# The last three and first two key tiles of a group summed bank by bank, and token ids and half of the first z loaded on ScalarE's queue

## The chip, the cores and the metric

The kernel runs on one core of a Trainium2 chip. The metric is the device time of one execution in microseconds (us). The kernel before takes 3062.32 us, the median of three runs (3061.7 to 3063.84). The execution that was profiled took 3063.57 us; its trace spans 3061.9 us.

## The reference

A gated attention unit feeds a hash-routed mixture of experts. All arrays are float32, except the token ids (int64).

```python
# u, v: (8, 2496, 256); z: (8, 2496, 64)
scores = (1.0 / S) * np.matmul(z, z.transpose(0, 2, 1))
attn = np.maximum(scores, 0.0) ** 2
x = (u * np.matmul(attn, v)).reshape(B * S, D)

expert_idx = token_ids * 2654435761 % 8
for e in range(8):
    mask = expert_idx == e
    h = np.maximum(x[mask] @ w1[e], 0.0)     # w1[e]: 256 x 1024
    out[mask] = h @ w2[e]                    # w2[e]: 1024 x 256
```

## The kernel before

**Stages.** The first 1836 us are the attention, the rest are the experts. The order of instructions on every engine is the order of the program's text; no scheduler changes it.

**Attention.** A batch has 2496 rows: 19 key tiles of 128 rows and a last one of 64. Queries go in groups of four tiles, five groups to a batch, 40 groups in all. For one group, `scores` (L131) multiplies z by itself for one key tile (L136, one matmul of 512 columns), ScalarE and VectorE take turns with the ReLU (L141, L139) and write the tile `a`, and VectorE squares `a` in place (`square`, L145, operation L148). `attend` (L160, matmul L162) then multiplies one 128-column piece of `a` by the 256 columns of `v` and adds it into `acc`. The scores of a group come in two parts: the first in the group before, just ahead of that group's last key tiles, the second at its own tile 7. The short key tile has a function of its own (`attend_last`, L157).

**The accumulators.** `acc` is two tiles of 128 x 2 x 256 floats, each one bank of PSUM, and there are two buffers for all groups. Queries q = 0 and 1 share the first bank, q = 2 and 3 the second. Once all 20 key tiles are added for a query, `gate` (L165, operation L171) has VectorE read its half of the bank, scale it, multiply it by `u` and write `x_sb`; after the fourth, GpSimd stores the rows to `x_rows` in device memory (L103).

**The end of a group.** Key tiles 0 to 15 are added for all four queries, tile by tile. For the last three (`LATE = 3`) the order turns round, query by query:

```python
for q in range(G):
    for t, a in late:
        attend(b, t, a, acc, [q])
    gate(b, g, q, acc)
    square(2)
    if q:
        between()
```

Matmuls and gates on one bank wait for each other: a gate waits for its query's last matmul, and the next matmul into that bank waits for the gate.

**The routing.** `places` (L187) works out from the token ids where each token goes. It is a generator; `between` (L342), called after every key tile, runs one step of it, so its VectorE operations sit between the squares. Its first step loads the ids to `tok` (L193, L194) on SyncE's queue, its mask (L224) feeds six small matmuls `cnt_ps` (L238) on TensorE, and a scan over 1280 columns follows (L243).

**Start of the program.** SyncE's queue issues, in this order: z of batch 0 twice, once into each half of `zn` (`load_z`, L108, six transfers), v and u of batch 0, z and v of batch 1 (`zn` has one buffer, so this waits for the transposes of batch 0), then the token ids. TensorE transposes z (L128), ScalarE copies the results to `zT` (L129), and the first scores follow.

**Experts.** Rows are gathered from `x_rows` (L414), multiplied by w1 and w2 (L433, L444) and scattered to the output (L447).

Of the kernel before, what the change touches and what calls it, by code (L numbers as in the profile page):

```python
# [12 lines left out]
I32 = mybir.dt.int32  # L13
# [11 lines left out]
def kernel(  # L25
# [10 lines left out]
    nc = tc.nc  # L36

    B, S, D = u.shape
    K = z.shape[-1]
    N = B * S  # L40
    E, _, F = moe_w1.shape
# [3 lines left out]
    P = 128  # L45
    TM = S // P
    SM = TM * P
    R = S - SM
    T = TM + 1
    assert R == 64 and K == 64  # L50
    G = 4
# [10 lines left out]
    def pool(name, bufs, **kw):  # L62
        return ctx.enter_context(tc.tile_pool(name=name, bufs=bufs, **kw))

    const = pool("const", 1)
# [19 lines left out]
    def width(t):  # L85
        return P if t < TM else R

    def group(g):
        return range(g * G, min(T, g * G + G))

    def tiles_io(dram, b, tiles, sb, store, eng, twice=False):

        rows = dram[ds(b * S, S), :]
        whole = [t for t in tiles if t < TM]
        pairs = []
        if whole:
            n = len(whole)
            pairs.append((rows[0:SM, :].rearrange("(p t) d -> p t d", t=TM)[:, ds(whole[0], n), :], sb[:, 0:n, :]))
        if TM in tiles:
            for i in range(2 if twice else 1):  # L100
                pairs.append((rows[SM:S, :], sb[ds(i * R, R), len(whole), :]))
        for d, s in pairs:
            eng.dma_start(out=d if store else s, in_=s if store else d)  # L103

    uf, vf, zf = (x.rearrange("b s d -> (b s) d") for x in (u, v, z))
    zn, zT, v_sb, u_sb, x_sb, made, to_square = {}, {}, {}, {}, {}, {}, []

    def load_z(b):  # L108
        zn[b] = npool.tile([P, T, 2, K], F32, name="zn")
        for i in range(2):  # L110
            tiles_io(zf, b, range(T), zn[b][:, :, i, :], False, nc.sync, twice=True)

    def load_v(b):
        v_sb[b] = vpool.tile([P, T, D], F32, name="v_sb")
        for g in range(NG):
            tiles_io(vf, b, group(g), v_sb[b][:, g * G:, :], False, nc.sync, twice=True)

    def load_u(b, g):
        u_sb[b, g] = upool.tile([P, G, D], F32, name="u_sb")
        tiles_io(uf, b, group(g), u_sb[b, g], False, nc.sync)  # L120

    def turn_z(b, g):

        if g == 0:
            zT[b] = zpool.tile([P, T * P], F32, name="zT")
        ps = mm_ps.tile([P, G * P], F32, name="z_ps", tag="mm")
        for i, t in enumerate(group(g)):
            nc.tensor.transpose(ps[:, ts(i, P)], zn[b][:, t].rearrange("p h k -> p (h k)"), ident[:])  # L128
        nc.scalar.copy(zT[b][:, ts(g, G * P)], ps[:])  # L129
# [15 lines left out]
    def square(n):  # L145
        for key in to_square[:n]:
            a = made[key]
            nc.vector.tensor_mul(a[:], a[:], a[:])  # L148
        del to_square[:n]
# [10 lines left out]
    def attend(b, t, a, acc, queries):  # L160
        for i in queries:
            nc.tensor.matmul(acc[i // 2][:, i % 2, :], a[:, ts(i, P)], v_sb[b][:, t, :],  # L162
                             start=(t == 0 and i % 2 == 0), stop=(t == TM - 1), skip_group_check=True)

    def gate(b, g, i, acc):  # L165
        q = g * G + i
        m = width(q)
        if i == 0:
            x_sb[b, g] = xpool.tile([P, G, D], F32, name="x_sb")
        x = x_sb[b, g]  # L170
        nc.vector.scalar_tensor_tensor(  # L171
            out=x[0:m, i, :], in0=acc[i // 2][0:m, i % 2, :], scalar=c2, in1=u_sb[b, g][0:m, i, :],
            op0=OP.mult, op1=OP.mult,
        )
        if i == G - 1:
            tiles_io(x_dram, b, group(g), x, True, nc.gpsimd)
# [7 lines left out]
    token = const.tile([P, B, T], I32)  # L184
    none = const.tile([P, NS], I32)

    def places():  # L187

        with tc.tile_pool(name="route", bufs=1) as route:
            tok_h = dataclasses.replace(moe_token_ids.tensor, shape=list(moe_token_ids.tensor.shape))  # L190
            tok_w = tok_h.bitcast(I32).rearrange("(b s two) -> b s two", b=B, two=2)
            tok = route.tile([P, B, T, 2], I32)
            nc.sync.dma_start(tok[:, :, 0:TM, :], tok_w[:, 0:SM, :].rearrange("b (p t) two -> p b t two", t=TM))  # L193
            nc.sync.dma_start(tok[0:R, :, TM, :], tok_w[:, SM:S, :].rearrange("b p two -> p b two"))  # L194

            iota_e = route.tile([P, E], F32)
            nc.gpsimd.iota(iota_e[:], pattern=[[1, E]], base=0, channel_multiplier=0,
                           allow_small_or_imprecise_dtypes=True)
# [29 lines left out]

            total = route.tile([P, E, C], F32)
            rank = route.tile([P, E, C], F32)
            H = 512 // C
# [87 lines left out]
    def slots_to_read():  # L321

        nc.vector.tensor_scalar(gidx[:], idx[:], float(N - 1), None, op0=OP.min)

    order = tc.manual_schedule()
    order.__enter__()

    load_z(0)
    load_v(0)
    load_u(0, 0)  # L330
    for g in range(NG):
        turn_z(0, g)

    LATE = 3
    parts = [[TM, *range(T // 2 - 1)], [*range(T // 2 - 1, TM)]]
    groups = [(b, g) for b in range(B) for g in range(NG)]
    place = places()
    i = 0  # L340

    def between():  # L342

        nonlocal i
        if i < 2 * T:
            next(place, None)
        elif i % 4 == 0 and i < 2 * T + 4 * C:
            enter((i - 2 * T) // 4)
        elif i == 2 * T + 4 * C + T:
            slots_to_read()  # L350
        i += 1
# [4 lines left out]
    for n, (b, g) in enumerate(groups):  # L356
        if n + 1 < len(groups):
            load_u(*groups[n + 1])
        if g == 0 and b + 1 < B:
            load_z(b + 1)  # L360
            load_v(b + 1)
            turns = iter(range(NG))

        def turn():
            k = next(turns, None) if g and b + 1 < B else None
            if k is not None:
                turn_z(b + 1, k)

        acc = [acc_ps.tile([P, 2, D], F32, name="acc", tag="acc") for _ in range(2)]
        for t in range(TM - LATE):  # L370
            if t == T // 2 - LATE:
                turn()
                scores(b, g, parts[1])
                attend_last(b, made.pop((b, g, TM)), acc)
                square(2)
                between()
            attend(b, t, made.pop((b, g, t)), acc, range(G))
            square(2)
            between()
        turn()  # L380
        if n + 1 < len(groups):
            scores(*groups[n + 1], parts[0])
        square(1)
        late = [(t, made.pop((b, g, t))) for t in range(TM - LATE, TM)]
        for q in range(G):
            for t, a in late:
                attend(b, t, a, acc, [q])
            gate(b, g, q, acc)
            square(2)
            if q:  # L390
                between()
    assert next(place, None) is None and i > 2 * T + 4 * C + T


# [104 lines left out]
```

## Time and profile before

| what | value |
|---|---|
| median of three runs | 3062.32 us |
| time of the profiled execution | 3063.57 us |
| its span | 3061.9 us |
| TensorE busy | 2981.1 us (97%) |
| VectorE busy | 1017.9 us (33%) |
| ScalarE busy | 428.1 us (14%) |
| GpSimd busy | 548.9 us (18%) |
| granted TensorE clock, mean | 0.996 |

In the trace one float32 matmul is two records of TensorE: the 40 x 76 calls of L162 are 6080 records. PE is TensorE's matmuls, PEld its weight loads, DVE is VectorE, ACT ScalarE, POOL GpSimd, and SPq is SyncE's queue of DMA issues. Ends of matmuls are modelled, so the time between two starts tells more than a group's own length. The granted clock is 1.00 at 2.4 GHz and 0.50 at 1.2 GHz.

### The profile page before, as it was taken

What the parts mean: (1) busy time and instruction counts of PE and PEld (TensorE: products, weight loads), DVE (VectorE), ACT (ScalarE), POOL (GpSimd) and SP (SyncE); (2) the same over time, 40 slices, a digit from 0 to 9 for tenths busy, and PEclk for the clock granted to TensorE, in tenths of its full rate; (3) what the DMA queues carried; (4) which work ended last, traced back from release to release, by engine and by line L of the source; (5) the groups of instructions that cost most, each with busy time, mean ns of one, the idle gap of its engine ahead of it and who ended that gap; (6) DMA issues with size and microseconds to landing.
All of it is one profiled execution on the core that took longest, in us unless ns stands there. A gap on an engine that the chain in (4) does not pass through costs nothing.

```text
span 3061.9 us, 33981 instructions
## 1 busy us (share of the span) xinstructions
PE 2981.1 (97%) x13946; PEld 2412.0 (79%) x13946; DVE 1017.9 (33%) x1649; ACT 428.1 (14%) x781; POOL 548.9 (18%) x564
## 2 busy tenths in 40 slices
PE   7999999999999999999999999999999999999999
PEld 5777777777777777777777778888888888888888
DVE  5544344454444444444445441111111111111111
ACT  1111111111111111111111111111111111111111
POOL 0011111011011011011100002223223222222232
PEclk9999999999999999999999999999999999999999
DMA  4011011011011011011000204545545545555453
GB/s 127 27 45 55 20 45 62 14 45 62 14 45 61 14 45 61 14 45 62 26 17 27 102 13 137 198 175 183 193 171 190 186 175 197 178 180 196 172 189 98
DMA packets 195547, 295.99 MB, mean 97 GB/s; under 512 B 59484, under 2 KB 148205, under 8 KB 195392
## 3 DMA queue, kind: packets, MB, share of 16 engines
q1 hardware_dynamic: 168400, 230.43, 23.1%
q0 software_dynamic: 26992, 63.39, 5.6%
q8 instruction: 110, 1.80, 0.2%
q14 instruction: 45, 0.37, 0.0%
HBM read 252.69 MB, written 42.90 MB: 97 GB/s over the span
## 4 chain that ended last, share of the span: by engine, by line
PE 64%; issue 24%; POOL 7%; DVE 3%; SPq 1%; DMA 1%; POOLq 0%; DVEq 0%
PE acc L162 40%; PE s_ps L136 11%; PE h_ps L433 6%; PE o_ps L444 5%; POOL xg L414 4%; POOL out_dram L447 3%; DVE x_sb L171 2%; DVE a L148 1%; PE acc L157 1%; SPq L103 1%; PE z_ps L128 0%; PE x_ps L423 0%; DMA tok<-in_moe_token_ids_dram 0%; POOLq L447 0%; DMA v_sb<-in_v_dram 0%
## 5 line engine op out<-in xcount | busy, mean ns | idle before, releaser
L162 PE MATMUL acc<-v_sb,a 128*128 128x256 f32 x6080 | 1357.3, 382 | 52.2 <-DVE x_sb L171 50.8
L162 PEld LDWEIGHTS acc<-v_sb,a 128*128 128x128 f32 x6080 | 1142.9, 190 | 277.3 <-DVE x_sb L171 82.9
L433 PE MATMUL h_ps<-xT,w 128*128 128x256 f32 x2720 | 617.0, 380 | 0.8 <-issue 0.8
L444 PE MATMUL o_ps<-w,hT 128*128 128x256 f32 x2720 | 614.5, 379 | 0.0
L139 DVE TENSOR_SCALAR a<-s_ps 128x512 f32<-128x512 f32 x400 | 276.6, 691 | 923.3 <-PE s_ps L136 923.3
L444 PEld LDWEIGHTS o_ps<-w,hT 128*128 128x128 f32 x2720 | 516.8, 190 | 70.3
L433 PEld LDWEIGHTS h_ps<-xT,w 128*128 128x128 f32 x2720 | 511.6, 191 | 67.7 <-issue 1.2
L148 DVE TENSOR_TENSOR a<-a 128x512 f32<-128x512 f32 x800 | 501.0, 683 | 0.0
L439 DVE TENSOR_SCALAR hT<-h_ps 128x512 f32<-128x512 f32 x170 | 117.6, 692 | 767.5 <-PE h_ps L433 767.5
L136 PE MATMUL s_ps<-zT 64*128 64x512 f32 x1600 | 365.6, 600 | 0.7 <-ACT zT L129 0.7
L141 ACT ACTIVATE a<-s_ps 128x512 f32<-128x512 f32 x400 | 238.8, 597 | 907.7 <-PE s_ps L136 907.7
L447 POOL DMA_INDIRECT out_dram<-o_sb,idx x170 | 170.7, 1004 | 819.8 <-ACT o_sb L446 807.8
L103 POOL DMA_DIRECT2D x_rows<-x_sb x48 | 27.7, 578 | 1582.3 <-DVE x_sb L171 1582.3
L136 PEld LDWEIGHTS s_ps<-zT 64*128 64x128 f32 x1600 | 148.3, 187 | 172.9 <-issue 171.7
L414 POOL DMA_INDIRECT xg<-x_rows,gidx x170 | 174.8, 1028 | 57.1 <-PE h_ps L433 28.5
L312 POOL DMA_INDIRECT slot_tokens<-token,addr x160 | 171.9, 1074 | 48.8 <-issue 48.8
L446 ACT COPY o_sb<-o_ps 128x256 f32<-128x256 f32 x170 | 63.2, 372 | 775.6 <-PE o_ps L444 775.6
L425 DVE COPY xT<-x_ps 128x512 f32<-128x512 f32 x85 | 58.8, 692 | 268.1 <-PE x_ps L423 268.1
L437 ACT ACTIVATE hT<-h_ps 128x512 f32<-128x512 f32 x170 | 101.5, 597 | 304.8 <-PE h_ps L433 269.6
L129 ACT COPY zT<-z_ps 128x512 f32<-128x512 f32 x40 | 23.3, 585 | 641.1 <-PE z_ps L128 641.1
L171 DVE SCALAR_TENSOR_TENSOR x_sb<-acc,u_sb 128x256 f32<-128x256 f32 (+1 forms) x160 | 67.6, 423 | 57.3 <-PE acc L162 57.3
L423 PE MATMUL x_ps<-ident,xg 128*128 128x128 f32 x340 | 51.8, 275 | 6.5 <-DMA xg<-x_rows,gidx 6.5
(54 smaller groups left out, 190.8 us busy)
## 6 DMA issues: line engine op xcount, KB each, us to landing
w<-in_moe_w_dram SPq DMA_DIRECT2D x170, 1024.0 KB
v_sb<-in_v_dram SPq DMA_DIRECT2D x32, 512.0 KB
u_sb<-in_u_dram SPq DMA_DIRECT2D x32, 512.0 KB
x_rows<-x_sb POOLq DMA_DIRECT2D x32, 512.0 KB
zn<-in_z_dram SPq DMA_DIRECT2D x16, 608.0 KB
v_sb<-in_v_dram SPq DMA_DIRECT2D x8, 384.0 KB
u_sb<-in_u_dram SPq DMA_DIRECT2D x8, 384.0 KB
x_rows<-x_sb POOLq DMA_DIRECT2D x8, 384.0 KB
```

The lines of the kernel that those rows point to most:

```text
L136: nc.tensor.matmul(ps[:], zT[b][h, ts(t, P)], zT[b][h, ts(g, G * P)], start=True, stop=True)
L139: nc.vector.tensor_scalar_max(a[:], ps[:], 0.0)
L141: nc.scalar.activation(a[:], ps[:], AF.Relu)
L148: nc.vector.tensor_mul(a[:], a[:], a[:])
L162: nc.tensor.matmul(acc[i // 2][:, i % 2, :], a[:, ts(i, P)], v_sb[b][:, t, :], start=(t == 0 and i % 2 == 0), stop=(t == TM - 1), skip_gro ...
L171: nc.vector.scalar_tensor_tensor(out=x[0:m, i, :], in0=acc[i // 2][0:m, i % 2, :], scalar=c2, in1=u_sb[b, g][0:m, i, :], op0=OP.mult, op1= ...
L312: st = nc.gpsimd.indirect_dma_start(out=slot_dram[:, None], out_offset=bass.IndirectOffsetOnAxis(ap=addr[0:n, c:c + 1], axis=0), in_=token ...
L414: nc.gpsimd.indirect_dma_start(out=xg[j][t][:], out_offset=None, in_=x_dram[:, :], in_offset=bass.IndirectOffsetOnAxis(ap=gidx[:, j * TB + ...
L433: nc.tensor.matmul(ps[:, i, :], w1[j][:, c, ts(f + i, P)], xT[j][:, c, :], start=(c == 0), stop=(c == DP - 1))
L439: nc.vector.tensor_scalar_max(o, ps[:], 0.0)
L444: nc.tensor.matmul(ps[:], hT[j][:, f, ts(t, P)], w2[j][:, f, :], start=(f == 0), stop=(f == FP - 1))
L447: st = nc.gpsimd.indirect_dma_start(out=out[:], out_offset=bass.IndirectOffsetOnAxis(ap=idx[:, j * TB + t:j * TB + t + 1], axis=0), in_=o[ ...
```

## The change

The last three key tiles are added in two passes, one for each bank: three tiles for queries 0 and 1, their two gates, then three tiles for queries 2 and 3 and their gates. The first two key tiles of the next group (`EARLY = 2`) are added in the same way, both tiles for queries 0 and 1, then both for 2 and 3. `square(1)` ahead of the last tiles becomes `square(3)`. The token ids are loaded right behind the first loads, on ScalarE's queue, and so is the second copy of z of batch 0. `places` gets six empty steps ahead of its first matmul.

```diff
-            tiles_io(zf, b, range(T), zn[b][:, :, i, :], False, nc.sync, twice=True)
+            tiles_io(zf, b, range(T), zn[b][:, :, i, :], False, nc.scalar if i and not b else nc.sync, twice=True)
...
+    def load_tokens():
...
+        nc.scalar.dma_start(tok[:, :, 0:TM, :], tok_w[:, 0:SM, :].rearrange("b (p t) two -> p b t two", t=TM))
+        nc.scalar.dma_start(tok[0:R, :, TM, :], tok_w[:, SM:S, :].rearrange("b p two -> p b two"))
...
-            nc.sync.dma_start(tok[:, :, 0:TM, :], tok_w[:, 0:SM, :].rearrange("b (p t) two -> p b t two", t=TM))
-            nc.sync.dma_start(tok[0:R, :, TM, :], tok_w[:, SM:S, :].rearrange("b p two -> p b two"))
...
+            for _ in range(6):
+                yield
             total = route.tile([P, E, C], F32)
...
     load_u(0, 0)
+    load_tokens()
...
+    EARLY = 2
     LATE = 3
...
-        for t in range(TM - LATE):
+        early = [(t, made.pop((b, g, t))) for t in range(EARLY)]
+        for k in range(2):
+            for t, a in early:
+                attend(b, t, a, acc, [2 * k, 2 * k + 1])
+            square(2)
+            between()
+        for t in range(EARLY, TM - LATE):
...
-        square(1)
+        square(3)
+
         late = [(t, made.pop((b, g, t))) for t in range(TM - LATE, TM)]
-        for q in range(G):
+        for k in range(2):
             for t, a in late:
-                attend(b, t, a, acc, [q])
-            gate(b, g, q, acc)
+                attend(b, t, a, acc, [2 * k, 2 * k + 1])
+            for q in (2 * k, 2 * k + 1):
+                gate(b, g, q, acc)
             square(2)
-            if q:
-                between()
+            between()
+        between()
```

**A group's end, TensorE.** One row here is one matmul of the program (two records in the trace), `x12` is twelve of them, and the words in brackets are what the first of them waits for (DVE: VectorE). Before, the 12 matmuls of the last three tiles and the first tiles of the next group stand so:

```order
L162 MATMUL acc<-v_sb,a 128x256 x3
L162 MATMUL acc<-v_sb,a 128x256 [waits DVE_49]
L162 MATMUL acc<-v_sb,a 128x256 x5
L162 MATMUL acc<-v_sb,a 128x256 [waits DVE_49]
L162 MATMUL acc<-v_sb,a 128x256 x4
L162 MATMUL acc<-v_sb,a 128x256 [waits DVE_49]
L162 MATMUL acc<-v_sb,a 128x256 x25
```

Now:

```order
L162 MATMUL acc<-v_sb,a 128x256 x12
L162 MATMUL acc<-v_sb,a 128x256 [waits DVE_49]
L162 MATMUL acc<-v_sb,a 128x256 x3
L162 MATMUL acc<-v_sb,a 128x256 [waits DVE_49]
L162 MATMUL acc<-v_sb,a 128x256 x15
```

The waits of query 1 and query 3 are gone from among the twelve; the waits for VectorE now stand ahead of the next group's first four matmuls (first bank) and its second four (second bank).

**The same place, VectorE.** The rows are the last ReLUs (L139), squares (L148) and gates (L171). Before, in the third group:

```order
L139 TENSOR_SCALAR a<-s_ps 128x512 x5
L148 TENSOR_TENSOR a<-a 128x512
L171 SCALAR_TENSOR_TENSOR x_sb<-acc,u_sb 128x256
L148 TENSOR_TENSOR a<-a 128x512 x2
L171 SCALAR_TENSOR_TENSOR x_sb<-acc,u_sb 128x256
L148 TENSOR_TENSOR a<-a 128x512 x2
L171 SCALAR_TENSOR_TENSOR x_sb<-acc,u_sb 128x256
L148 TENSOR_TENSOR a<-a 128x512 x2
L171 SCALAR_TENSOR_TENSOR x_sb<-acc,u_sb 128x256
L148 TENSOR_TENSOR a<-a 128x512 x3
```

Now in the very first group, where the routing's steps run too (L247 is the scan, L250 and L252 an addition and a subtraction over 1280 columns):

```order
L139 TENSOR_SCALAR a<-s_ps 128x512 x5
L148 TENSOR_TENSOR a<-a 128x512 x3
L171 SCALAR_TENSOR_TENSOR x_sb<-acc,u_sb 128x256 x2
L148 TENSOR_TENSOR a<-a 128x512 x2
L247 SCALAR_TENSOR_TENSOR upto<-ones,total 128x1280
L171 SCALAR_TENSOR_TENSOR x_sb<-acc,u_sb 128x256 x2
L148 TENSOR_TENSOR a<-a 128x512 x2
L250 TENSOR_TENSOR rank<-rank,upto 128x1280
L252 TENSOR_TENSOR rank<-rank,total 128x1280
```

The gates come in pairs with two squares between the pairs. In the first group alone the scan has moved between the pairs; it stood ahead of that group's last ReLUs before.

**The start, TensorE and ScalarE.** TensorE before:

```order
L136 MATMUL s_ps<-zT 128x512 x10
L162 MATMUL acc<-v_sb,a 128x256 x24
L238 LDWEIGHTS all_230
L238 MATMUL cnt_ps<-mask,all_230 128x480
L162 MATMUL acc<-v_sb,a 128x256 x4
L238 LDWEIGHTS below
L238 MATMUL cnt_ps<-mask,below 128x480
L136 MATMUL s_ps<-zT 128x512 x10
```

Now:

```order
L136 MATMUL s_ps<-zT 128x512 x10
L162 MATMUL acc<-v_sb,a 128x256 x28
L136 MATMUL s_ps<-zT 128x512 x10
L157 MATMUL acc<-v_sb,a 128x256 x4
L162 MATMUL acc<-v_sb,a 128x256 x16
L242 LDWEIGHTS all_230
L242 MATMUL cnt_ps<-mask,all_230 128x480
```

And ScalarE now, whose first instruction was the table load before:

```order
L103 DMA zn<-in_z_dram 128x19x64
L103 DMA zn<-in_z_dram 64x64 x2
L192 DMA tok<-in_moe_token_ids_dram 128x8x38
L193 DMA tok<-in_moe_token_ids_dram 64x8x2 [waits DMAHW0_49]
L129 ACT_TABLE_LOAD
L129 COPY zT<-z_ps 128x512 [waits PE_49] x5
```

The first routing matmul moves from behind 24 matmuls of L162 to behind 44 and the second part of the scores. ScalarE issues five transfers ahead of its table load and its first copy, and the fifth waits for an earlier transfer, the first of z.

## Rows read from the trace of the kernel before

**Rows 1.** Windows of the two stages: PE, PEld, DVE, ACT, POOL busy, clock, DMA, GB/s.
```profile
60.00:1836.00 1776.00, 1724.85 (x7983) 1312.91 (x7981) 812.65 (x1351) 253.31 (x425) 199.67 (x208) 1.00 0.13 40
1836.00:3061.90 1225.90, 1214.69 (x5780) 1068.36 (x5780) 176.40 (x256) 164.74 (x340) 346.11 (x341) 1.00 0.50 176
```
**Rows 2.** Who waited for whom: us in total, times, longest.
```profile
PE acc L162 <- DVE x_sb L171: 50.8, 80, 0.8
```
**Rows 3.** Timeline of TensorE over one group: start, us, what, [idle before it].
```profile
250.17 1.56 PE L162 MATMUL acc<-v_sb,a 128*128 128x256 f32 x6
...
269.45 4.56 PE L136 MATMUL s_ps<-zT 64*128 64x512 f32 x20
...
274.80 15.81 PE L162 MATMUL acc<-v_sb,a 128*128 128x256 f32 x72
290.54 4.56 PE L136 MATMUL s_ps<-zT 64*128 64x512 f32 x20
```
**Rows 4.** Timeline of TensorE and VectorE at the end of a later group.
```profile
1788.49 1.56 PE L162 MATMUL acc<-v_sb,a 128*128 128x256 f32 x6
...
1789.24 0.68 DVE L148 TENSOR_TENSOR a<-a 128x512 f32<-128x512 f32 x1
1790.09 0.42 DVE L171 SCALAR_TENSOR_TENSOR x_sb<-acc,u_sb 128x256 f32<-128x256 f32 x1 [0.17 <-PE acc L162]
...
1790.57 2.86 PE L162 MATMUL acc<-v_sb,a 128*128 128x256 f32 x12 [0.52 <-DVE x_sb L171]
...
1793.71 0.42 DVE L171 SCALAR_TENSOR_TENSOR x_sb<-acc,u_sb 128x256 f32<-128x256 f32 x1
1794.04 1.28 DVE L148 TENSOR_TENSOR a<-a 128x512 f32<-128x512 f32 x2
...
1794.18 13.65 PE L162 MATMUL acc<-v_sb,a 128*128 128x256 f32 x62 [0.76 <-DVE x_sb L171]
```
**Rows 5.** Timeline of TensorE at the last group's end.
```profile
1813.12 17.10 PE L162 MATMUL acc<-v_sb,a 128*128 128x256 f32 x78
...
1834.11 1.56 PE L162 MATMUL acc<-v_sb,a 128*128 128x256 f32 x6 [0.52 <-DVE x_sb L171]
```
**Rows 6.** Timeline of the start, all engines.
```profile
0.82 1.28 ACT L129 ACT_TABLE_LOAD   x1 [0.82 <-PEq L485]
...
9.37 3.76 PE L128 MATMUL z_ps<-ident,zn 128*128 128x128 f32 x20 [9.37 <-DMA zn<-in_z_dram]
...
12.20 1.60 ACT L129 COPY zT<-z_ps 128x512 f32<-128x512 f32 x3 [0.27 <-PE z_ps L128]
...
19.84 10.63 PE L162 MATMUL acc<-v_sb,a 128*128 128x256 f32 x48 [1.42 <-DVE a L148]
...
28.09 1.70 SPq L194 DMA_DIRECT2D tok<-in_moe_token_ids_dram  x1
...
37.43 0.56 PE L238 MATMUL cnt_ps<-mask,all 128*128 128x480 bf16 x1 [6.97 <-DVE mask L224]
...
46.71 1.03 PE L157 MATMUL acc<-v_sb,a 64*128 64x256 f32 x8
...
49.60 0.37 PE L238 MATMUL cnt_ps<-mask,below 128*128 128x480 bf16 x1
...
55.50 2.81 DVE L243 TENSOR_TENSOR_SCAN upto<-ones,total 128x1280 f32<-128x1280 f32 x1
```
**Rows 7.** Chain that ended last, SyncE's issue of the second z.
```profile
4.18 0.60 SPq L103
```
**Rows 8.** Windows of the start; the last three columns: granted clock, DMA share, GB/s.
```profile
2.00:9.37 7.37, 0.00 (x0) 0.03 (x1) 0.00 (x0) 0.11 (x1) 1.80 (x5) 1.00 0.99 193
5.00:6.00 1.00, 0.00 (x0) 0.00 (x0) 0.00 (x0) 0.00 (x0) 0.00 (x0) 1.00 0.48 103
7.00:8.00 1.00, 0.00 (x0) 0.00 (x0) 0.00 (x0) 0.00 (x0) 0.00 (x0) 1.00 1.33 250
33.00:36.00 3.00, 0.00 (x0) 0.00 (x0) 1.02 (x5) 0.00 (x0) 0.00 (x0) 0.50 0.74 206
```

More of the change, by code (lines that the diff above doesn't have):

```diff
@@ L185 @@
     none = const.tile([P, NS], I32)
+    tok = const.tile([P, B, T, 2], I32)
+    def load_tokens():
+        tok_h = dataclasses.replace(moe_token_ids.tensor, shape=list(moe_token_ids.tensor.shape))
+        tok_w = tok_h.bitcast(I32).rearrange("(b s two) -> b s two", b=B, two=2)
+        nc.scalar.dma_start(tok[:, :, 0:TM, :], tok_w[:, 0:SM, :].rearrange("b (p t) two -> p b t two", t=TM))
+        nc.scalar.dma_start(tok[0:R, :, TM, :], tok_w[:, SM:S, :].rearrange("b p two -> p b two"))
     def places():
         with tc.tile_pool(name="route", bufs=1) as route:
-            tok_h = dataclasses.replace(moe_token_ids.tensor, shape=list(moe_token_ids.tensor.shape))
-            tok_w = tok_h.bitcast(I32).rearrange("(b s two) -> b s two", b=B, two=2)
-            tok = route.tile([P, B, T, 2], I32)
-            nc.sync.dma_start(tok[:, :, 0:TM, :], tok_w[:, 0:SM, :].rearrange("b (p t) two -> p b t two", t=TM))
-            nc.sync.dma_start(tok[0:R, :, TM, :], tok_w[:, SM:S, :].rearrange("b p two -> p b two"))
             iota_e = route.tile([P, E], F32)
```

## The prediction

> **What bounds the kernel now.** I read the windows of the two stages first, then who waits for whom, then the timeline at the places the change touches. In the attention stage TensorE's matmuls are busy 1724.85 of 1776 us at full granted clock, VectorE 812.65; in the experts' stage 1214.69 of 1225.9 [rows 1]. So TensorE sets the end in both, and only time in which it waits can be won. The experts' stage has almost none and is not touched. In the list of waits the large one is matmuls into `acc` waiting for gates: 80 times, two for each of the 40 groups [rows 2].
>
> Its price is better read from starts, because ends of matmuls are modelled. Inside a group 72 records take 290.54 - 274.80 = 15.74 us, 0.2186 each [rows 3]. From the first late matmul at 250.17 to the next scores at 269.45 stand 80 records (24 of the last three tiles, 56 of tiles 0 to 6), which at that pace need 17.49 us. They take 19.28. **1.79 us** of each group is lost at its end [rows 3].
>
> A later group shows how. Query 0's six records start at 1788.49, the gate at 1790.09, and query 1, in the same bank, starts at 1790.57. Query 3 starts at 1794.18, after a gate at 1793.71 that had squares ahead of it on VectorE [rows 4]. Query 2, in the other bank, waits for nothing: it is inside the group of twelve.
>
> The start has a second hole. TensorE stands 6.97 us until the routing's mask is there [rows 6], and the granted clock in that hole is 0.50, which is 1.2 GHz [rows 8], so what follows is slow as well.
>
> **The gates.** From rows 4 I take: a block of n records ends n x 0.2186 + 0.25 after its start (six: 1.56), its gate starts 0.04 later and lasts 0.42, the next VectorE operation starts 0.33 after a gate's start (1793.71 to 1794.04), TensorE resumes 0.05 after a gate's end (1794.13 to 1794.18), two squares take 1.28, each 0.61 behind the one before. Let T be the first late matmul (1788.49). VectorE begins its squares at T + 0.75 and with three of them is free at 2.65. The new order then gives:
> - the first bank's 12 records end at 2.87; gates at 2.91 and 3.25; two squares from 3.58 to 4.86;
> - the second bank's 12 records start at 2.62, with no wait, and end at 5.50; VectorE has been free for 0.68; gates at 5.54 and 5.87, the last ends at 6.29, and its bank is open at 6.34;
> - meanwhile the next group's first 8 records run in the first bank from 5.25, open since 3.72, on tiles squared by 2.65; the next 8 need the second bank at T + 32 x 0.2186 = 7.00.
>
> That leaves 0.65 us to spare, and the loss is nothing: 39 x 1.79 = **69.8 us** gained. This rests on the cover of the next group's first 8 records (1.75 us); with one early tile it would be half, and some 0.2 us of wait would stay. The number of matmuls, weight loads, squares and gates is unchanged. Bounds: a wait that is already met costs between nothing and the 0.05 of a resume, so up to 80 x 0.05 = 4 us; my pitch may be off by 0.05 us a group, 2 us either way.
>
> **The last group** has no next one. Its 96 records from 1813.12 would end unhindered at 1834.36; they end at 1835.67 [rows 5]: 1.31 us. The second gate of the pair now comes 0.33 later, and the larger store of rows, which before left ahead of the last matmuls, leaves behind them. I take **0.7**, between 0 and 1.0.
>
> **The hole at the start.** From the first L162 at 19.84, 56 records (28 matmuls, 12.24 us) and 20 of scores (4.56, the modelled length of the same group in [rows 3]) would bring the short key tile to 36.64. It comes at 46.71 [rows 6]: 10.1 us, the wait and the slow clock together. Two of the routing's matmuls move behind that point and return; I charge half of their 0.37 each [rows 6], as part lies beside other matmuls. That leaves **9.7 us**. It needs the token ids before TensorE has 44 more matmuls done, and they now leave ahead of v and z of batch 1 rather than behind. The second transfer of ids costs up to 1.70 us of issue [rows 6], now on ScalarE's queue.
>
> **z on two queues.** The first transpose waits for z until 9.37 [rows 6]; the second z's first transfer is issued at 4.18 [rows 7] and can leave at about 0.9 now. Between 2.00 and 9.37 the DMA engines show a mean share of 0.99, with 0.48 from 5 to 6 and 1.33 at their busiest [rows 8]. At 1.33 throughout, the same traffic takes 7.37 x 0.99 / 1.33 = 5.5 us and z lands at 7.5, 1.9 earlier. But ScalarE must then finish its queue: the last id transfer waits for the first z, is issued in up to 1.70, and the table load of 1.28 follows [rows 6], so the first copy of z^T starts at up to 10.5 and the fifth, 0.53 each, ends at 13.1. Before, it ended at 13.80 [rows 6]. Gain 0.7 with that slow issue, 1.9 at best; I take **1.0**. If z lands no earlier than 9.37, ScalarE's queue makes it 15.0, a loss of 1.2.
>
> Here a rule speaks against the change. The Trainium skill, "DMA: Bandwidth & Descriptors", section "Issuing engines are not separate DMA queues", says that transfers issued from several engines run on the same 16 DMA engines and that only the sequencer's issue time is saved, which it calls usually small. By it only the dip from 5 to 6 would be filled, some 0.6 us as an estimate, z would land at 8.7, ScalarE would end at 14.3, and the term would be -0.5 instead of +1.0, the sum 78.2.
>
> **Worth nothing.** SyncE's queue loses two id transfers and three of z, so v of batch 0 and u of the second group are issued some 2 to 3 us earlier; at 19.84 the first matmul waits for a square, not for v [rows 6], and u is read only by a gate 50 us later. The six empty steps move the routing's VectorE work later: its last step, the addresses, comes at the end of the second group, and GpSimd's scatter of ids starts in the third as before.
>
> **The scan** is the one thing that gets worse. In the first group its 2.81 us [rows 6] now stand between the two pairs of gates: free at 4.86 + 2.81 = 7.67, the last gate ends at 8.42, the bank opens at 8.47 instead of by 7.00. **-1.5 us**, between 0 and the whole 2.8. In the second group a short step stands there, inside the 0.65 to spare; from the third on nothing does.
>
> **The sum.** 69.8 + 0.7 + 9.7 + 1.0 - 1.5 = 79.7 us. The profiled execution took 3063.57, which gives 2983.9; the median of the runs lies 1.25 below the profiled one, so 2982.6, which I round to **2983 us**.
>
> **The rivals.**
> - *A wait behind the squares.* The next group's second bank waits not for the last gate but for the two squares behind it: 6.20 + 1.28 = 7.48, resumed at 7.53, 0.54 late in each of 39 groups, 21 us: **3003**. Against it: query 3 resumes at 1794.18 while the squares issued at 1794.04 still run [rows 4]. For it: the margin is only 0.65. Chance 0.07.
> - *The ids are still late.* If the transfer on ScalarE's queue lands as late as before, the hole stays and only the gates' part comes: **2992**. Against it: it is ahead of most other traffic, and the first routing matmul has moved some 13 us later. Chance 0.06.
> - *Each switch of bank waits for both gates (slower).* If the late matmuls of the second bank waited for the first bank's gates, they would start at 3.67 + 0.05 = 3.72 instead of 2.62, 1.10 late; and if the next group's first bank waited for the second's gates, another 1.10. That is 2.20 a group in place of 1.79: 39 x 0.41 = 16 us lost against 9 won at the start: **3069**. It decides from 2.03 us a group upward. Against it: query 2 does not wait for query 1's gate now, and the 62 records from 1794.18 hold the next group's first matmuls without a break [rows 4]; the new order of instructions shows twelve matmuls with no wait among them. Chance 0.02.
>
> **How the numbers follow.** The forecast has 0.83, the rivals 0.07, 0.06 and 0.02, and 0.02 are left for what I don't see. Its own bounds run from 2976 (z 0.9 better, no scan stall, last group 0.3, pitch 2, and some 2 for the hole) to 2993 (met waits 4, z 2.2 worse, scan 1.3, last group 0.7, pitch 2). The range 2976 to 2996 takes in the second rival, and leaves out the first and the third. About 0.2%, 6 us, is what a measurement of this kernel can tell from no change: every case but the slower one and part of the unseen lies far beyond it on the fast side, so faster 0.97, same 0.01, slower 0.02.
>
> **What would show it.** Right: the list of waits has no 80-fold row of `acc` matmuls waiting for gates, at most one of about 1.5 us in the first group; from the first late matmul to the next scores a group takes 17.5 us; no wait for the mask and no 0.50 clock near 33 us; the short key tile of the first group near 36 us; the attention stage ends near 1757 us and the experts' stage stays at 1226. Wrong: a wait for a gate at every group's ninth early record, a hole at the routing's first matmul, or an experts' stage that changes.

## The result and the profile after

The change takes **2985.44 us**, the median of four runs (2984.54 to 2987.51), against 3062.11 for the kernel before beside it (3061.7 to 3063.84): a ratio of 0.975, interval 0.9733 to 0.9766. The forecast was 2983, its range 2976 to 2996. The profiled execution took 2984.54 with a span of 2982.9, so the two spans differ by 79.0 us; the sum of the prediction was 79.7. The medians differ by less, 76.7 us: the profiled execution of the change is the shortest of its four, and that of the kernel before, 3063.57, lies 1.5 above the median beside it.

The list of waits first (us in total, times, longest), a row of the changed kernel:

```profile
PE acc L162 <- DVE x_sb L171: 1.1, 1, 1.1
```

The 80-fold row of [rows 2] is gone. One wait for a gate is left, 1.1 us, and no row names the routing's mask any more. The windows of the two stages, cut where the attention now ends (columns as in [rows 1]):

```profile
60.00:1758.00 1698.00, 1694.83 (x7944) 1314.11 (x7942) 810.55 (x1349) 250.68 (x421) 205.52 (x209) 1.00 0.14 41
1758.00:2982.90 1224.90, 1213.98 (x5780) 1067.88 (x5780) 176.28 (x255) 164.85 (x340) 345.84 (x340) 1.00 0.51 176
```

In [rows 1] TensorE's matmuls left 51.15 of 1776 us idle in the attention stage; now it is 3.17 of 1698. The experts' stage is as it was.

Now a group's end, from the timeline of the changed kernel (start, us, what, idle before it). The first two rows are one steady group and the scores behind it; the rest is the end of another:

```profile
192.29 17.53 PE L162 MATMUL acc<-v_sb,a 128*128 128x256 f32 x80
209.75 2.42 PE L136 MATMUL s_ps<-zT 64*128 64x512 f32 x10
```
```profile
278.39 13.87 PE L162 MATMUL acc<-v_sb,a 128*128 128x256 f32 x63
...
281.29 0.76 DVE L171 SCALAR_TENSOR_TENSOR x_sb<-acc,u_sb 128x256 f32<-128x256 f32 x2 [0.26 <-PE acc L162]
281.96 1.28 DVE L148 TENSOR_TENSOR a<-a 128x512 f32<-128x512 f32 x2
283.88 0.75 DVE L171 SCALAR_TENSOR_TENSOR x_sb<-acc,u_sb 128x256 f32<-128x256 f32 x2 [0.64 <-PE acc L162]
```

The 80 records from the first late matmul to the next scores take 209.75 - 192.29 = 17.46 us in place of 19.28 [rows 3], and stand in one row without a break. With T = 278.39 the gates come at T + 2.90 and the second pair at T + 5.49; the forecast had 2.91 and 5.54. VectorE waits 0.26 and 0.64 for TensorE ahead of the pairs, and TensorE waits for neither.

The start, from TensorE's timeline of the changed kernel:

```profile
9.47 4.50 PE L128 MATMUL z_ps<-ident,zn 128*128 128x128 f32 x20 [9.47 <-DMA zn<-in_z_dram]
14.65 4.56 PE L136 MATMUL s_ps<-zT 64*128 64x512 f32 x20 [0.68 <-ACT zT L129]
20.63 12.35 PE L162 MATMUL acc<-v_sb,a 128*128 128x256 f32 x56 [1.42 <-DVE a L148]
...
37.31 1.03 PE L157 MATMUL acc<-v_sb,a 64*128 64x256 f32 x8
...
45.28 0.37 PE L242 MATMUL cnt_ps<-mask,all 128*128 128x480 bf16 x1
...
59.58 7.17 PE L162 MATMUL acc<-v_sb,a 128*128 128x256 f32 x32
67.86 10.63 PE L162 MATMUL acc<-v_sb,a 128*128 128x256 f32 x48 [1.11 <-DVE x_sb L171]
```

The hole ahead of the routing is closed: from the first L162 to the short key tile stand 37.31 - 20.63 = 16.68 us, before 26.87 [rows 6]. But z landed at 9.47, not earlier than before, its 20 transposes take 4.50 instead of 3.76 [rows 6], and the first L162 stands at 20.63 instead of 19.84: here this execution lost 0.8 us, most of it by the slower transposes, whose pace differs between executions of one kernel (last section). The one wait for a gate is that of the first group, where VectorE's timeline shows the scan between the two pairs:

```profile
62.47 0.76 DVE L171 SCALAR_TENSOR_TENSOR x_sb<-acc,u_sb 128x256 f32<-128x256 f32 x2 [0.26 <-PE acc L162]
63.15 1.28 DVE L148 TENSOR_TENSOR a<-a 128x512 f32<-128x512 f32 x2
64.35 2.82 DVE L247 TENSOR_TENSOR_SCAN upto<-ones,total 128x1280 f32<-128x1280 f32 x1
67.08 0.73 DVE L171 SCALAR_TENSOR_TENSOR x_sb<-acc,u_sb 128x256 f32<-128x256 f32 x2
```

The end of the last group, from TensorE's timeline of the changed kernel:

```profile
1734.96 20.99 PE L162 MATMUL acc<-v_sb,a 128*128 128x256 f32 x96
1763.14 0.66 PE L437 MATMUL x_ps<-ident,xg 128*128 128x128 f32 x2 [7.19 <-DMA xg<-x_rows,gidx]
```

Its 96 records end at 1755.95 without a stall. But the first rows of the experts are waited for 7.19 us; in the trace of before the same wait is 6.00.

### The profile page after: what moved, and what is told of

It is laid out like the page before. It is cut to its first block, busy times and chain, and to the rows that moved or that the text cites. A ratio compares the mean times of both kernels' runs of the same rounds, so it can differ in the third digit from the quotient of the medians.

```text
span 2982.9 us, 33985 instructions
## 1 busy us (share of the span) xinstructions
PE 2957.2 (99%) x13946; PEld 2417.5 (81%) x13946; DVE 1014.6 (34%) x1649; ACT 428.4 (14%) x781; POOL 554.5 (19%) x564
## 4 chain that ended last, share of the span: by engine, by line
PE 56%; issue 33%; POOL 10%; POOLq 0%; DMA 0%; DVE 0%; ACT 0%
PE acc L162 42%; PE s_ps L136 12%; POOL xg L428 6%; POOL out_dram L461 4%; PE acc L157 1%; PE z_ps L128 1%; DMA zn<-in_z_dram 0%; POOLq L461 0%; POOLq L428 0%; DVE upto L247 0%; DMA x_rows<-x_sb 0%; DVE x_sb L171 0%; DVE a L148 0%; POOLq L508 0%; PE cnt_ps L242 0%
## 5 line engine op out<-in xcount | busy, mean ns | idle before, releaser
L162 PE MATMUL acc<-v_sb,a 128*128 128x256 f32 x6080 | 1334.7, 380 | 2.5 <-DVE a L148 1.4
L162 PEld LDWEIGHTS acc<-v_sb,a 128*128 128x128 f32 x6080 | 1148.5, 190 | 199.8 <-issue 42.8
L139 DVE TENSOR_SCALAR a<-s_ps 128x512 f32<-128x512 f32 x400 | 276.6, 692 | 861.8 <-PE s_ps L136 861.8
L148 DVE TENSOR_TENSOR a<-a 128x512 f32<-128x512 f32 x800 | 494.6, 684 | 0.0
L171 DVE SCALAR_TENSOR_TENSOR x_sb<-acc,u_sb 128x256 f32<-128x256 f32 (+1 forms) x160 | 60.3, 419 | 48.3 <-PE acc L162 48.3
```

The source lines that it names most:

```text
L139: nc.vector.tensor_scalar_max(a[:], ps[:], 0.0)
```

## The experiments

**One part at a time.** The change has two halves that need not go together: the order of the key tiles, and the loads with the six empty steps. The first kernel has the new order alone, the second all but the new order (no early tiles bank by bank, the late ones query by query).

```diff
# e1_banks_only: the kernel before, with
+     EARLY = 2
...
+        for k in range(2):
+            for t, a in early:
+                attend(b, t, a, acc, [2 * k, 2 * k + 1])
...
# e2_start_only: the change, with
-        for t in range(EARLY, TM - LATE):
+        for t in range(TM - LATE):
...
-        for k in range(2):
+        for q in range(G):
             for t, a in late:
-                attend(b, t, a, acc, [2 * k, 2 * k + 1])
...
+                attend(b, t, a, acc, [q])
+            gate(b, g, q, acc)
```

> The kernel before with the two passes over the banks alone (last three and first two key tiles); ids, z and the empty steps as before. Theory (the terms add up, each in its own place): the 39 group ends give 39 x 1.8 = 70 us, the hole of 7 us ahead of the routing's first matmul stays, the scan does not stand between the gates: 2991 to 2993 us. Rival (the hole and the group ends are tied, the hole goes once TensorE needs the mask at another time): 2983. Rival (banks alone gain nothing without the earlier loads): 3062.

> The change without the passes over the banks: ids and half of z on ScalarE's queue and the six empty steps stay, key tiles in the order of before. Theory: the hole (7 us and the slow clock behind it, about 10 us) goes, z is not earlier (about 0.8 lost), the scan stands in front of a gate (1 to 2 lost): 3053 to 3056 us, 80 waits of about 0.6 us for gates stay in the list. Rival (terms tied): 3062.

The new order alone takes 2991.63 us (2990.88 to 2992.39), ratio 0.9769 (0.9754 to 0.9784): 70.9 below 3062.53, inside the expectation, with the hole where it was. TensorE's timeline of that kernel:

```profile
37.29 0.56 PE L238 MATMUL cnt_ps<-mask,all 128*128 128x480 bf16 x1 [6.61 <-DVE mask L224]
```

The loads and empty steps alone take 3058.76 us (3057.73 to 3059.93), ratio 0.9989 (0.998 to 0.9998), some 3 us more than expected. TensorE's and VectorE's timelines of that kernel in the first group say why:

```profile
67.14 15.14 PE L162 MATMUL acc<-v_sb,a 128*128 128x256 f32 x62 [3.47 <-DVE x_sb L171]
```
```profile
63.95 2.82 DVE L247 TENSOR_TENSOR_SCAN upto<-ones,total 128x1280 f32<-128x1280 f32 x1
66.69 0.40 DVE L171 SCALAR_TENSOR_TENSOR x_sb<-acc,u_sb 128x256 f32<-128x256 f32 x1
```

The scan, moved into the group's end, stands ahead of a gate that the old order waits for at once: that wait is 3.47 us, in an old group 0.76 [rows 4]. From its first late matmul at 58.73 to the transposes at 82.11 the group takes 23.38 us, 4.1 more than an old group's 19.28. The longer wait is 2.7 of them. The rest comes behind it, as that kernel's windows show (granted clock third from the end):

```profile
64.00:67.00 3.00, 0.00 (x0) 0.00 (x0) 3.00 (x3) 0.00 (x0) 0.00 (x0) 0.96 0.00 0
67.00:70.00 3.00, 2.86 (x7) 2.32 (x8) 2.69 (x4) 0.00 (x0) 0.00 (x0) 0.50 0.00 0
```

After the wait the granted clock is 0.50 (1.2 GHz), and the 62 records take 67.14 to 82.11 = 14.97 us in place of 62 x 0.2186 = 13.55: 1.4 us.

When the experts begin, 5.4 us of the gain at the start are left (their first matmul stands at 1838.95, before at 1844.37). The two spans differ by 4.5, because the experts' stage is 0.9 longer in this execution; in the traces of all the kernels here it lasts 1216.85 to 1218.45 us, so that is scatter. The medians differ by 3.8. So the two halves help each other: the loads and empty steps are worth 5.8 to 6.2 us with the new order (the first by differences to the kernel before, 76.7 - 70.9, the second by medians of separate batches, 2991.63 - 2985.44) and 3.8 without it.

**How much cover the gates need.** Of the new order, too, there are two parts. One kernel adds only one key tile bank by bank ahead of the others; one adds two so, but the late tiles query by query as before.

```diff
# e3_one_early_tile: the change, with
-    EARLY = 2
+    EARLY = 1
...
-            square(2)
-            between()
+            if k:
+                square(2)
+                between()
# e8_early_alone: the change, with
-        square(3)
+        square(1)
...
-        for k in range(2):
+        for q in range(G):
             for t, a in late:
-                attend(b, t, a, acc, [2 * k, 2 * k + 1])
...
+                attend(b, t, a, acc, [q])
+            gate(b, g, q, acc)
```

> The changed kernel with one early key tile in place of two, squares and routing steps at the same count. Theory (the next group's first records in the other bank cover the pair of gates): the second bank is needed 28 records = 6.12 us after the first late matmul and opens at 6.24 + 0.05 by the gates of the changed kernel: 0.1 to 0.25 us of wait in each of 39 groups, seen as some 39 waits for gates, 2989 to 2995 us. Rival (the late passes alone do it, the early tiles are idle): no such waits, 2985.

> The changed kernel with the last three key tiles query by query as before; the two early tiles stay in passes over the banks. Theory (the two waits of a group stand within the late tiles; the early tiles only cover the pair of gates that the late passes make): 80 waits for gates stay, 3053 to 3059 us, like the kernel with the start alone. Rival (the early tiles bring the gain): near 2985.

With one early tile: 2996.46 us (2995.11 to 2997.37), ratio 0.9785 (0.977 to 0.98), 11.0 above the change. The rows of that kernel's list of waits and of its timeline at the end of a group:

```profile
PEld acc L162 <- DVE x_sb L171: 14.3, 32, 2.4
PE acc L162 <- DVE x_sb L171: 2.0, 1, 2.0
```
```profile
286.90 0.76 DVE L171 SCALAR_TENSOR_TENSOR x_sb<-acc,u_sb 128x256 f32<-128x256 f32 x2 [0.63 <-PE acc L162]
...
287.70 2.46 PEld L162 LDWEIGHTS acc<-v_sb,a 128*128 128x128 f32 x12 [0.39 <-DVE x_sb L171]
```

The weight load of the second bank's first matmul waits for the second pair of gates; TensorE's matmul row shows no break there, as ends of matmuls are modelled, so the price is read from starts: the group from 106.84 takes 17.62 us to the transposes at 124.46, in the change 17.37 (104.88 to 122.25). That is 0.25 us x 38 = 9.5 us. The first group takes 21.30 us (58.99 to 80.29) instead of 18.75, 2.55 more: its wait is 1.98 instead of 1.11, and behind it the granted clock reads 0.56 from 67 to 70 and 0.87 from 70 to 73, where the change has 1.00 from 65 to 74. Less 0.6 by which the sums start earlier in this execution, that makes 11.5 of the 11.8 us between the two spans. The prediction had "some 0.2 us of wait would stay"; the expectation's upper end, 2995, was 1.5 too low, because it had no price for the first group.

With two early tiles but the old order of the late ones: 3058.64 us (3057.42 to 3060.2), ratio 0.9987 (0.9977 to 0.9996), inside the expectation, and what the kernel without any of the new order gives (3058.76). Its row of waits is the old one:

```profile
PE acc L162 <- DVE x_sb L171: 53.6, 80, 3.5
```

So the early tiles alone gain nothing. They are the cover for the last gates, and without the pairs of late queries the waits stand among the late tiles, where no early tile reaches. The pairs with no early tile at all were not run.

**The two smaller terms.** One kernel moves the second copy of z back to SyncE's queue; one puts one empty step more ahead of the scan.

```diff
# e4_z_on_sync: the change, with
-            tiles_io(zf, b, range(T), zn[b][:, :, i, :], False, nc.scalar if i and not b else nc.sync, twice=True)
+            tiles_io(zf, b, range(T), zn[b][:, :, i, :], False, nc.sync, twice=True)
# e5_scan_later: the change, with, ahead of the scan,
+            yield
```

> The changed kernel with the second half of the first z back on SyncE's queue; the ids stay on ScalarE's. Theory (the 16 DMA engines bound z, two queues only interleave): z lands at 9.2 to 9.8 us as before, first matmul of the sums at 19.8 to 20.6, total within 1 us of the changed kernel. Rival (two queues bring z earlier and something else ate it): z lands 1 us or more later than 9.47 and the total is 1 to 2 us longer.

> The changed kernel with one more empty step ahead of the scan, so that it stands behind the second pair of gates. Theory (the scan holds the pair back, 1.3 us once): the one wait for a gate in the first group goes, from the first late matmul to the next z transposes the first group takes 17.4 us in place of 18.75, total 1 to 1.5 us shorter, 2984. Rival (the scan is paid in any place): the wait turns up elsewhere, total unchanged.

z on one queue: 2985.66 us (2985.25 to 2988.25), ratio 0.975 (0.9737 to 0.9764). Against the change's 2985.44 that is no difference. But the expectation of the start was missed: z landed at 10.31, later than its 9.2 to 9.8, and the first L162 stands at 23.32. The scan a step later: 2983.3 us (2982.45 to 2984.65), ratio 0.9742 (0.9728 to 0.9755). Its wait for a gate in the first group is gone from TensorE's timeline:

```profile
59.19 17.53 PE L162 MATMUL acc<-v_sb,a 128*128 128x256 f32 x80
76.56 0.60 PE L128 MATMUL z_ps<-ident,zn 128*128 128x128 f32 x4
```

That group takes 17.37 us, in the change 78.33 - 59.58 = 18.75: 1.4 us, and 2.1 between the two medians, which were taken in separate batches of runs.

**Why an earlier z is worth nothing.** If the load itself is the limit, half the load must help. So z is loaded once and VectorE copies it to the other half of `zn`; then the same with the later scan.

```diff
# e6_z_once: the change, with
-        for i in range(2):
+        for i in range(1 if b == 0 else 2):
...
+        if b == 0:
+            nc.vector.tensor_copy(zn[b][:, :, 1, :], zn[b][:, :, 0, :])
# e7_scan_and_z: this and the empty step of e5_scan_later
```

> The changed kernel with z of batch 0 loaded once, on SyncE's queue, and copied to the other half of the tile by VectorE. Theory (z's landing is bound by what the 16 DMA engines move, not by the queue): half the traffic, z lands at 5 to 6 us and with the copy the first transpose starts at 6.5 to 8 in place of 9.47; total 2 to 3 us shorter, 2982.5 to 2983.5. Rival (landing is set by a fixed latency or by issue): first transpose at 9 or later, no gain.

> Both of the two edits before in one kernel. Theory: they add up, 3 to 4.5 us shorter than the changed kernel, 2981 to 2982.5. Rival: each gain is within the spread of the starts, nothing is seen in the median.

They took 2984.65 us (2983.77 to 2986.43), ratio 0.9744 (0.9731 to 0.9757), and 2984.13 (2981.16 to 2984.24), ratio 0.9739 (0.9726 to 0.9753): both medians miss their expectation by about 1 to 2 us. Half the traffic did bring z sooner, but less than expected: VectorE's copy starts at 7.42 (6.0 at the latest was expected) and the first transpose at 8.35 (6.5 to 8). TensorE's timeline of the first shows an earlier start that is lost before the first L162 (its line numbers are 2 higher; L164 is L162):

```profile
8.35 4.50 PE L130 MATMUL z_ps<-ident,zn 128*128 128x128 f32 x20 [8.35 <-DVE zn L113]
13.53 6.53 PE L138 MATMUL s_ps<-zT 64*128 64x512 f32 x20 [0.67 <-ACT zT L131]
21.48 12.35 PE L164 MATMUL acc<-v_sb,a 128*128 128x256 f32 x56 [1.42 <-DVE a L150]
```

z is ready 1.1 us sooner, the first L162 comes 0.9 later. The 20 scores take 6.53 us instead of 4.56. No wait is longer than in the change; TensorE itself is slower. The theory formed here: it does its first matmuls slowly, whenever they come, and an earlier z only moves that stretch forward. If so, matmuls that nobody reads, done while z is on its way, should bring the pace up. The next kernels put identity transposes into a bank of their own ahead of those of z; the change itself ran beside them once more.

```diff
# e10_scan_warm: e5_scan_later, with
+    warm = mm_ps.tile([P, G * P], F32, name="warm_ps", tag="mm")
+    for i in range(48):
+        nc.tensor.transpose(warm[:, ts(i % G, P)], ident[:], ident[:])
# e11_scan_z_warm: the same added to e7_scan_and_z
# e12_scan_z_warm34: e11_scan_z_warm, with
-    for i in range(48):
+    for i in range(34):
```

> The changed kernel once more, on the same chip as the two below, to compare them with: 2984 to 2987 us; the first matmul of the sums between 19.8 and 23 us, as the starts have differed in the runs so far.

> The kernel with the scan one step later, and 48 transposes of the identity, read by nobody, on TensorE ahead of the first transposes of z. Theory (the start differs from run to run because TensorE's first matmuls after its idle start run at half pace for a while, and that eats what z's landing gives): the 20 transposes of z take 2 to 3 us in place of 4.5, the first scores 4.56, the first matmul of the sums comes at 18 to 19.2, total 2980.5 to 2982.5. Rival (pace of the first transposes is set by z's data, not by idleness): 4.5 us and 20 or later, no gain.

> The same with z of batch 0 loaded once and copied by VectorE. Theory: with TensorE at full pace the 1.1 us by which z is there earlier is no longer eaten: the first matmul of the sums at 16.8 to 18.2, total about 1 us below the kernel with the 48 transposes alone, 2979.5 to 2981.5. Rival: the earlier z is eaten elsewhere, no difference between the two.

The change again: 2986.85 us (2985.3 to 2987.34), ratio 0.9752 (0.9738 to 0.9765). With the later scan and 48 transposes: **2981.8 us** (2981.28 to 2982.74), ratio 0.9737 (0.9724 to 0.9751), 5.0 below the change on the same chip. The scan's step is part of that (1.4 us by the traces above); a kernel with the extra transposes alone was not run, and against the later scan alone (2983.3, a separate batch) the total is 1.5 lower. TensorE's timeline of the kernel with the transposes:

```profile
1.52 7.07 PE L335 MATMUL warm_ps<-ident 128*128 128x128 f32 x48 [1.52 <-POOL ident masks.py:199]
9.01 2.37 PE L128 MATMUL z_ps<-ident,zn 128*128 128x128 f32 x20 [0.42 <-DMA zn<-in_z_dram]
12.27 4.56 PE L136 MATMUL s_ps<-zT 64*128 64x512 f32 x20 [0.89 <-ACT zT L129]
18.25 12.35 PE L162 MATMUL acc<-v_sb,a 128*128 128x256 f32 x56 [1.42 <-DVE a L148]
```

The transposes of z take 2.37 us instead of 4.50, and the first L162 stands at 18.25, in the change on that chip at 22.03. The rival asked for 4.5 and 20 or later. With z loaded once as well (e11_scan_z_warm): 2982.16 us (2980.85 to 2982.99), ratio 0.9736 (0.9723 to 0.9749), no better, because the 48 extra transposes lasted until 9.75 and z, ready at 8.3, had to wait for them. The same 48 took 8.40 us here and 7.07 above. Neither its expected start, 16.8 to 18.2, was met (18.96) nor its total, 2979.5 to 2981.5. So there was a last one with 34:

> One z transfer with VectorE's copy, the scan a step later, and 34 instead of 48 identity transposes ahead of the transposes of z. Theory (z's early arrival is only worth something if TensorE is at full pace and free when it comes): the 34 end by 8.0, the transposes of z start at 8.3 to 8.5 and take 2.4, the first matmul of L162 comes at 17.4 to 17.8, and the total is 0.5 to 1 us below the version with 48 transposes and the doubled z (2981.8), so 2980.8 to 2981.5. Rival (34 are too few to bring TensorE to full pace): the transposes of z take 3 to 4.5, the first L162 comes at 19 or later, 2982.5 or more.

It takes **2980.58 us** (2980.05 to 2981.56), ratio 0.9734 (0.9721 to 0.9747), the fastest of all. TensorE's timeline:

```profile
1.52 5.27 PE L337 MATMUL warm_ps<-ident 128*128 128x128 f32 x34 [1.52 <-POOL ident masks.py:199]
8.29 2.40 PE L130 MATMUL z_ps<-ident,zn 128*128 128x128 f32 x20 [1.50 <-DVE zn L113]
...
17.56 12.35 PE L164 MATMUL acc<-v_sb,a 128*128 128x256 f32 x56 [1.42 <-DVE a L150]
```

The 34 end at 6.79, TensorE stands idle for 1.50 and keeps its pace. The first L162 at 17.56 is 0.69 earlier than with 48 transposes and the doubled z, as the theory had it; the rival asked for 19 or later. Its total is 0.2 below what was expected. The totals of the three differ by little more than their scatter, and the last was taken in a separate batch of runs, so the start in the trace speaks here, not the total, and it is that of one execution: in one as slow as that of e11_scan_z_warm the 34 would take longer.

## Why the prediction was right, and where it was not

By its own terms, in us gained, each measured between the two profiled executions:

| term | forecast | measured | from |
|---|---|---|---|
| gates, 39 groups | 69.8 | 70.5 | first group's first late matmul to the last group's long row of L162: 1744.64 (68.48 to 1813.12) to 1675.38 (59.58 to 1734.96), and the scan's 1.3 added back |
| last group | 0.7 | 0.2 | that row to the first experts' matmul: 31.25 (to 1844.37) to 31.09 (to 1766.05) |
| hole at the start | 9.7 | 9.7 | first L162 to first late matmul: 48.64 (19.84 to 68.48) to 38.95 (20.63 to 59.58) |
| z on two queues | 1.0 | -0.8 | first L162: 19.84 to 20.63 |
| scan | -1.5 | -1.3 | 67.86 less (59.58 + 32 x 0.2186) |
| experts | 0 | 0.7 | first experts' matmul to the end of the span: 1217.53 to 1216.85 |
| sum | 79.7 | 79.0 | the spans differ by 79.0 |

One of these starts is this row of TensorE's timeline of the kernel before:

```profile
68.48 1.56 PE L162 MATMUL acc<-v_sb,a 128*128 128x256 f32 x6
```

The sum holds for the two profiled executions. By the medians the change gains 76.7, and 2985.44 is 2.4 above the forecast, so the pair was partly luck: the 0.7 of the experts' stage is scatter (the change's 1216.85 us are the shortest of all the traces), and in the second trace of the change (e9_after_again) the first L162 stands 1.4 later, at 22.03.

**The gates** are shown: alone they give 70.9 us (70.6 by the same starts, 68.52 to 1742.52), and they need both parts, the pairs of late queries (without them 80 waits stay) and two early tiles (with one, 0.25 us a group come back). Half the cover was just too little and the whole was enough, as the steps from T had it. None of the rivals holds: no group waits for squares behind its gates, no switch of bank waits for the other bank's gates. The bound of 4 us for waits already met was too careful: a group is 0.03 shorter than 80 records of 0.2186.

**The hole** closed as forecast. The ids were in time by far: the first routing matmul, at 45.28, waits for nothing.

**The term that failed is z**: "At 1.33 throughout, the same traffic takes 7.37 x 0.99 / 1.33 = 5.5 us and z lands at 7.5". It landed at 9.47. The windows of the changed kernel up to there, and the timeline of its queues and of ScalarE:

```profile
2.00:9.47 7.47, 0.00 (x0) 0.03 (x1) 0.00 (x0) 0.90 (x1) 1.81 (x5) 1.00 1.21 210
5.00:6.00 1.00, 0.00 (x0) 0.00 (x0) 0.00 (x0) 0.00 (x0) 0.00 (x0) 1.00 1.37 218
```
```profile
0.83 3.69 ACTq L103 DMA_DIRECT2D zn<-in_z_dram  x3
0.83 5.54 SPq L103 DMA_DIRECT2D zn<-in_z_dram  x3
4.55 0.61 ACTq L192 DMA_DIRECT2D tok<-in_moe_token_ids_dram  x1
...
8.57 1.28 ACT L129 ACT_TABLE_LOAD   x1 [8.57 <-DMA zn<-in_z_dram]
10.60 0.59 ACT L129 COPY zT<-z_ps 128x512 f32<-128x512 f32 x1 [0.74 <-PE z_ps L128]
...
14.01 0.59 ACT L129 COPY zT<-z_ps 128x512 f32<-128x512 f32 x1 [0.27 <-PE z_ps L128]
```

The dip of [rows 8] between 5 and 6 is filled (1.37 in place of 0.48), and the share rose from 0.99 to 1.21. But the traffic is not the same: 7.47 us at 210 GB/s are 1.57 MB where 7.37 at 193 were 1.42, and 0.15 MB is about what the ids hold (8 x 2496 of 8 bytes). And a share of 1.21 moved 210 GB/s where 0.99 moved 193, so a byte cost more. The rule that the prediction set against this part, of the Trainium skill, "DMA: Bandwidth & Descriptors", section "Issuing engines are not separate DMA queues", says that transfers issued from several engines share the same 16 DMA engines. The traces agree in the main: with two queues z landed at 9.16 to 9.47 in six traces, with one queue and the ids far behind it at 9.37 and 9.59 in two. That the prediction's estimate by the rule, -0.5, lies near the measured -0.8 is luck: it had z at 8.7 and ScalarE as the limit behind it, and neither came. The run with z on one queue leaves a part open: there z landed at 10.31, 0.84 later than with two, so the second queue may well make up for what the ids cost. But in that kernel the ids leave at 0.83 and in the change at 4.55, these are single executions, and the totals show no difference.

The size of the loss is not the load's. z is 0.1 later than before; 0.7 of the 0.8 is the slow pace of the first matmuls, which the prediction did not have as a term at all. It let ScalarE set the pace behind z, at 0.53 a copy, although only the last three copies in [rows 6] stand so close. ScalarE's first copy starts at 10.60, almost where the prediction had it (10.5), and waits 0.74 for TensorE; the five then follow 0.85 apart, each waiting for the transposes, and end at 14.60, not 13.1. ScalarE's queue itself did no harm: from the start of the transposes to the first copy stand 1.13 us (9.47 to 10.60), before 1.12 (9.37 to 10.49).

Among the parts **worth nothing** a reading was off without harm: v of batch 0 begins to leave 1.0 earlier (6.42 against 7.45), not 2 to 3, and the first rows of u leave 1.35 later (12.63 against 11.28); no matmul waits for either.

**The last group** was mis-sized: 0.7 against 0.2. The matmuls end 1.56 sooner after the first late one, but the first rows of the experts are waited for 1.19 longer (7.19 against 6.00) and the next 0.22 longer (0.74 against 0.52), because the larger store leaves behind the last gate, at 1756.70, and the gather waits for it. The mechanism was named; the upper half of its range was not to be had.

**The scan** came out as worked out, and the run that moves it by one step gets it back.

## What to carry to other kernels

Where a reader and the next matmuls share a bank of an accumulator, order the work by banks and not by outputs: finish one bank's sums, read them while the other bank is filled, and count the cover in time, matmuls behind the last read against the read itself (eight records of 1.75 us were enough for a pair of gates of 0.76, four left 0.25 us per group). An earlier load is worth only what the engine behind it makes of it: look at the pace of its first instructions before pricing the load. A step that moves in one engine's program is priced at its new place; the same scan cost its group 4.1 us ahead of one gate and 1.4 ahead of another, and a third of the larger price was not the wait itself but the half clock behind it.

## What the runs showed of the hardware that was not expected

TensorE's first matmuls run at about half pace, and for how long differs from one execution to the next, though they are the same matmuls, and even in one kernel (the change and e9_after_again). From the timelines of all kernels, in us:

| kernel | z ready | 20 transposes | 20 scores | first L162 | z ready to first L162 |
|---|---|---|---|---|---|
| before | 9.37 | 3.76 | 4.56 | 19.84 | 10.47 |
| e2_start_only | 9.32 | 3.75 | 4.56 | 19.78 | 10.46 |
| e1_banks_only | 9.59 | 3.76 | 4.56 | 20.05 | 10.46 |
| e3_one_early_tile | 9.28 | 4.05 | 4.56 | 20.04 | 10.76 |
| e5_scan_later | 9.18 | 4.41 | 4.56 | 20.24 | 11.06 |
| the change | 9.47 | 4.50 | 4.56 | 20.63 | 11.16 |
| e9_after_again | 9.16 | 4.50 | 6.28 | 22.03 | 12.87 |
| e4_z_on_sync | 10.31 | 4.50 | 6.41 | 23.32 | 13.01 |
| e8_early_alone | 9.23 | 4.50 | 6.53 | 22.36 | 13.13 |
| e6_z_once | 8.35 | 4.50 | 6.53 | 21.48 | 13.13 |
| e7_scan_and_z | 8.31 | 4.50 | 6.64 | 21.55 | 13.24 |
| e10_scan_warm | 9.01 | 2.37 | 4.56 | 18.25 | 9.24 |
| e12_scan_z_warm34 | 8.29 | 2.40 | 4.56 | 17.56 | 9.27 |
| e11_scan_z_warm | 8.3, first transpose at 9.75 | 2.35 | 4.56 | 18.96 | 9.21 from 9.75 |

Without matmuls ahead the way from z to the first L162 takes 10.46 to 13.24 us, with them 9.24 and 9.27 where TensorE was free when z came. That is 1.2 to 4.0 us of loss and a scatter of 2.8 us, more than the whole z term. The windows of e10_scan_warm over its 48 extra transposes (the matmul count is in brackets behind the first busy time; then the granted clock) show the pace rise:

```profile
1.50:3.00 1.50, 1.48 (x7) 1.49 (x8) 0.00 (x0) 0.00 (x0) 1.43 (x7) 1.00 0.33 77
...
6.00:8.60 2.60, 2.58 (x24) 2.35 (x22) 0.00 (x0) 0.43 (x1) 0.00 (x0) 1.00 1.39 213
```

From 7 in 1.5 us (0.21 each) to 24 in 2.6 (0.11 each): a factor of 2, the ratio of the clock's two levels, 1.2 and 2.4 GHz. Yet the granted clock reads 1.00 in all these rows, at half the pace too, so this column alone does not show such a start. Where it does read 0.50, behind the wait of e2_start_only, records run at half pace too: 7 from 67.14 to 70.00, 0.41 each against 0.2186. The Trainium skill, "TensorE: Matmul & The Clock Gate", section "Part 1: The HAM clock gate (the "warmup" mystery)", says that the throttled rate is the default and that activity releases it. The paces agree with that, the column does not; that the clock is the cause is inferred from the factor and from what the extra transposes do, not read from a row. Why the slow stretch ends within the transposes in some executions and within the scores in others stays open.
